# Attention with routing in front of a mixture of experts: order of VectorE's work around a tile's normalisation, and gate logits summed on GpSimd

## The chip, the cores and the metric
The kernel runs on one core of one Trainium2 chip. The metric is device time in microseconds of one execution. Before the change it was 1285.98 us, the median of three runs (1285.92 to 1286.72). Engines: TensorE (PE; PEld is its weight load), VectorE (DVE), ScalarE (ACT), GpSimd (POOL), and SyncE (SP), which issues most DMAs.

## The reference
Three stages, all in float32:

```python
k_p = k.reshape(B, H, Sp, 8, D).mean(axis=3)      # B, H, S, D = 8, 8, 576, 64
v_p = v.reshape(B, H, Sp, 8, D).mean(axis=3)      # 72 pooled keys a head
attn = softmax(q @ k_p^T / 8);  x = attn @ v_p    # -> 4608 tokens x 512
skip = x @ w_skip                                 # only tokens with skip > 0 are computed
logits = x @ w_gate                               # 8 experts, the largest one is used
x += softmax(logits)[e] * (relu(x @ w1[e]) @ w2[e])
h = x @ w_in;  out = (h * sigmoid(h)) @ w_out     # 512 -> 2048 -> 512, all tokens
```

## The kernel before
The 4608 tokens are 36 tiles of 128. Attention runs over the tiles in one software-pipelined loop (i = 0 to 35); the experts' stage then works through units of up to 384 tokens of one expert, and the feed-forward stage through blocks of 512 tokens. Each engine executes its instructions in the order in which the program writes them; nothing is reordered. So the order of the Python statements in the loop is the order of each engine's queue.

In iteration i of the loop in `attention`:

- `products(i+3)`: TensorE makes the scores of a later tile (two PSUM banks, out of a ring of four: three of the pool `hp` and one more). `ptrans(i+1)` transposes the probabilities of the next tile; ScalarE copies them to `pts`. `scores(i+3)`: VectorE takes the row maximum (`mx`, twice), ScalarE makes eight exponentials (`prb`).
- `place(1, ...)`: GpSimd issues one indirect DMA that writes 128 token numbers to their slots (`slots`). It waits for the last instruction of ScalarE, and a second one at the end of the iteration for the last one of VectorE, as a pace.
- `ready`: one entry of the list `todo`, which holds the routing in steps. An entry has a TensorE part (`count`: a few small matmuls, `rps`, that count tokens of each expert, into a bank of `hp`), a VectorE part (`step1`, 8 operations; `step2`, 9; `choose`, 6; `early`, 3), and a number (A1, A2, A3) of operations that run ahead of the tile's normalisation. The rest runs behind it.
- `pv(i)`: TensorE multiplies the probabilities with the pooled values `vex`. The result has columns for the output, for the sum of the row, and for the nine logits of each head (eight gates and the skip score), in the one PSUM buffer `pv`.
- `post(i)`: VectorE adds 1e-9 to the row sums (`sm`), inverts them, scales the logits of each head (`cc`, 8 x 9 columns) and the outputs (`x`), and sums `cc` over the heads to `lg`. When `x` is done, `pv` is free for the next tile. SP stores `x`.
- `pool_k`: VectorE sums the keys of a later batch over eight positions, in four pieces (`kp`), in the tiles that `KEYS` lists: `2: (2,3,4,4)`, `3: (6,6,7,8)`, `4: (11,12,13,13)`, `5: (15,15,16,17)`, `6: (20,20,21,22)`, `7: (24,24,25,26)`. In the tile of the last piece, `keys` has ScalarE make `kbd` of it, which the score products read.
- `self.slow`: two operations an iteration of `keep_one`, from tile 30 on, which decide on a unit that is kept.
- `pool_v`: GpSimd sums the values of a later batch over eight positions (`v`, `v`, `vp`); `router1` has TensorE transpose the sums (`vtp`); `values` has GpSimd write `vex`; `router2` has TensorE multiply with the gate weights (`cps`) and VectorE write the result to `vex`.

The tiles form groups of 9, 9, 9, 6 and 3 (`GROUP`: group, place j in it, size n). After a group's last tile the logits are stored and the group is routed (`route`), its steps spread over the next iterations. In tiles 30, 31, 32 and 35 VectorE also makes `w1l`, for the experts; after tiles 34 and 35 TensorE transposes the first unit's tokens (`xtp`) and VectorE makes `xtl`, which the first expert product `hp` reads.

In the stage `moe`, ahead of the loop over units, the first unit's tokens are copied from `xn` to `xr` by `keep()` (one of three slices on ScalarE, two on VectorE in one instruction). Behind it on VectorE stand `low2(f)`, which make `w2l`, the low halves of the second weights, for the products `yp`.

Of the kernel before, what the change touches and what calls it, by code (L numbers as in the profile page):

```python
# [5 lines left out]
F32 = mybir.dt.float32  # L6
# [7 lines left out]
ALU = mybir.AluOpType  # L14
AX = mybir.AxisListType
# [3 lines left out]
P = 128  # L19
B, H, S, D = 8, 8, 576, 64  # L20
# [3 lines left out]
E, FM = 8, 1024  # L24
# [13 lines left out]
U = 3  # L38
# [4 lines left out]
KEYS = {2: (2, 3, 4, 4), 3: (6, 6, 7, 8), 4: (11, 12, 13, 13), 5: (15, 15, 16, 17), 6: (20, 20, 21, 22),  # L43
        7: (24, 24, 25, 26)}
# [8 lines left out]
OPS = [2, 2, 2, 0, 4, 4]  # L53
ORDER = list(range(NT // 512))[::-1]
SLOW = 2
A1, A2, A3 = 8, 5, 12

C_E, C_MV, C_LID, C_WT, C_THR, C_LE, C_UN, C_PK, C_TRI = 0, 2, 13, 49, 57, 153, 217, 241, 265
C_N = C_TRI + P
# [98 lines left out]
class Kern:  # L158
# [19 lines left out]
    def attention(self, xa, rs, extra):  # L178
        nc, tc, c = self.nc, self.tc, self.c
        self.todo = todo = []  # L180
        self.slow = iter(())
        with tc.tile_pool(name="as", bufs=1) as s1, \
# [31 lines left out]
            def pool_k(b, eng, halves=(0, 2), n=2):  # L214
                k = k_t[b]
                kp = st.get((b, "k"))
                if kp is None:
                    kp = st[b, "k"] = s2.tile([P, 4, G], F32, name=f"kp_{b}", tag="kp")
                if eng is nc.vector:
                    for a in halves:  # L220
                        eng.tensor_reduce(kp[:, a:a + n], k[:, a:a + n], AX.X, ALU.add)
                else:
                    eng.tensor_tensor(k[:, :, :, 0:4], k[:, :, :, 0:4], k[:, :, :, 4:8], ALU.add)
                    eng.tensor_tensor(k[:, :, :, 0:2], k[:, :, :, 0:2], k[:, :, :, 2:4], ALU.add)
                    eng.tensor_tensor(kp, k[:, :, :, 0], k[:, :, :, 1], ALU.add)
# [98 lines left out]
            def pv(t, pt):  # L324
                ps = pp.tile([P, 1024], F32, name=f"pv_{t}", tag="pv")
                ps = ps[:, 0:H * HW].rearrange("p (h e) -> p h e", e=HW)
                for i, j, h0, n, start, stop in PVS:
                    for b, o, r, m in parts(t):
                        ve = vex[b % NB]
                        nc.tensor.matmul(ps[r:r + m, h0:h0 + n, 0:VW], pt[:CP, i, r:r + m], ve[:CP, j:j + n],  # L330
                                         start=start, stop=stop, skip_group_check=True)
                st["pv"] = ps

            def post(t):
                ps = st.pop("pv")
                xr = self.x4[:, t % 4]
                sm = s2.tile([P, H], F32, name=f"sm_{t}", tag="sm")
                cc = s2.tile([P, H, E + 1], F32, name=f"cc_{t}", tag="cc")
                nc.vector.tensor_scalar(sm, ps[:, :, D], 1e-9, None, ALU.add)
                yield  # L340
                nc.vector.reciprocal(sm, sm)
                yield
                nc.vector.tensor_tensor(cc, ps[:, :, D + 1:VW], bc(sm, 2, E + 1), ALU.mult)
                yield
                nc.vector.tensor_tensor(xr[:, 0:DM].rearrange("p (h d) -> p h d", d=D), ps[:, :, 0:D],
                                        bc(sm, 2, D), ALU.mult)
                yield
                g, j, n = GROUP[t]
                if j == 0:
                    st["lg"] = rs.tile([P, 9, E + 1], F32, name=f"lg{g}", tag="lg")  # L350
                lg = st["lg"][:, j]
                nc.vector.tensor_reduce(lg, cc.rearrange("p h e -> p e h"), AX.X, ALU.add)
                yield
                nc.sync.dma_start(xa[P * t:P * (t + 1), 0:DM], xr[:, 0:DM])
                if j == n - 1:
                    nc.sync.dma_start(xa[P * (t - j):P * (t + 1), DM:XW].rearrange("(t p) e -> p t e", p=P),
                                      st["lg"][:, 0:n, 0:E])
                    self.route(rs, g, t - j, n, st["lg"][:, 0:n])
# [30 lines left out]
            for i in range(-2, NTILE):  # L389
                if i == -2:  # L390
                    pool_v(0, ON0)
                n = 3 if i > DEEP else 2
                if i > 0 and i + n < NTILE:
                    pss = products(i + n)
                    pts[i + 1] = ptrans(i + 1, prs.pop(i + 1))
                    prs[i + n] = scores(i + n, pss)
                elif i != -1 and i <= DEEP:
                    prs[i + 2] = scores(i + 2)
                if len(self.to_place) > (3 if i < EARLY else 0) and i < NTILE - 1:
                    self.place(1, nc.scalar.last)  # L400
                extra(i, True)
                ready = todo.pop(0) if todo and i < NTILE - 1 else None
                if ready and ready[0]:
                    ready[0]()
                if i == -2:
                    values(0)
                    loadv(1)
                    loadq(1)
                if i == -1:
                    pss = products(1)  # L410
                    router1(0)
                if i == 0:
                    pv(0, pts.pop(0))
                if 0 <= i + 1 < NTILE and i + 1 not in pts:
                    pts[i + 1] = ptrans(i + 1, prs.pop(i + 1))
                if i == -1:
                    prs[1] = scores(1, pss)
                    router2(0)
                    pool_k(1, nc.vector, (0,))
                    pool_v(1, ON1)  # L420
                    values(1)
                if i > 0:
                    pv(i, pts.pop(i))
                a = ready[1]() if ready and ready[1] else iter(())
                b = post(i) if i >= 0 else iter(())
                for _ in range(ready[2] if ready else 0):
                    next(a, None)
                for _ in range(SLOW):
                    next(self.slow, None)
                for bb, tiles in KEYS.items():  # L430
                    for r, t in enumerate(tiles):
                        if i == t:
                            pool_k(bb, nc.vector, (r,), 1)
                for _ in b:
                    pass
                for _ in a:
                    pass
                for bb, tiles in KEYS.items():
                    if i == tiles[-1]:
                        keys(bb)  # L440
                if i == 0:
                    pool_k(1, nc.vector, (2,))
                    keys(1)
                for b in range(B):
                    if i + 4 == first[b] and 0 < b < B - 1:
                        loadq(b + 1)
                    if 0 <= i + 2 - first[b] < 2 and 0 < b < B - 1:
                        pool_v(b + 1, 0, ((0,), (1, 2))[i + 2 - first[b]])
                    if i + 2 == first[b]:
                        if b + 2 < B:  # L450
                            loadk(b + 2)
                            loadv(b + 2)
                    if i + 2 == first[b] + 3 + (b == 0) and b + 1 < B:
                        router1(b + 1)
                    if i + 2 == first[b] + 3 and 0 < b < B - 1:
                        values(b + 1)
                    if i + 2 == first[b] + 5 and b + 1 < B:
                        router2(b + 1)
                if i == DEEP:
                    prs[i + 3] = scores(i + 3)  # L460
                if i == EARLY + 7:
                    self.read_table(nc.sync)
                if i == 2:
                    nc.sync.dma_start(self.cb, self.con[:, P + C_TRI:])
                if i == 6:
                    self.consts()
                if i < NTILE - 1:
                    self.place(1, nc.vector.last)
                else:
                    self.place(len(self.to_place))  # L470
                extra(i)
# [373 lines left out]
    def moe(self, xa, up):  # L845
        nc, tc, c = self.nc, self.tc, self.c
        with tc.tile_pool(name="ms", bufs=1) as s1, \
             tc.tile_pool(name="mw", bufs=2) as s2, \
             tc.tile_pool(name="mp", bufs=2, space=PSUM) as pp:
            raw2, xn, xth, xtl, gi, si = self.raw2, self.xn, self.xth, self.xtl, self.gi, self.si  # L850
# [3 lines left out]
            xr = s1.tile([P, U, XW], F32, name="xr", tag="xr")  # L854
            y = self.x4[:, 0:U]

            def keep():
                nc.scalar.copy(xr[:, U - 1], xn[:, U - 1])
                nc.vector.tensor_copy(xr[:, 0:U - 1], xn[:, 0:U - 1])
# [76 lines left out]
            count, places, _ = self.todo.pop(0)  # L936
# [12 lines left out]
            def low2(f):  # L949
                nc.vector.tensor_tensor(self.w2l[:, f], raw2[:, f], self.w2h[:, f].bitcast(F32), ALU.subtract)  # L950

            keep()
            for f in range(4):
                low2(f)
            while not next(units):
# [67 lines left out]
            with tc.For_i(0, nu, 1, iteration_sync="reg_based") as u:  # L1023
                ld = lambda i, o, hi: nc.value(self.ut[0:1, i, bass.ds(u + o, 1)], hi)
                e = ld(0, 1, E - 1)
                self.load_w1(e)
                keep()
                n = ld(2, 0, U * P)
# [51 lines left out]
            for s in (2, 1):  # L1080
# [3 lines left out]
                while done:  # L1084
                    f = done.pop(0)
# [6 lines left out]
            while done:  # L1092
                f = done.pop(0)
# [560 lines left out]
```

## Time and profile before
| what | value |
|---|---|
| median of three runs | 1285.98 us (1285.92 to 1286.72) |
| the profiled execution's own time | 1285.66 us |
| its span | 1283.9 us |
| granted TensorE clock, mean | 0.997 |
| TensorE busy | 1244.5 us (97%) |
| VectorE busy | 850.9 us (66%) |
| ScalarE busy | 576.4 us (45%) |
| GpSimd busy | 354.8 us (28%) |
| attention, tiles 0 to 35 | about 19 to 151 us of the span |
| first unit of the experts' stage | about 149 to 189 us |

The profile is of one execution. Busy times are sums over instructions; an idle time carries the name of what ended it. The share over the whole span says little about attention, in which all engines are busier than on average. The chain that ended last runs through TensorE in the stages after attention.

### The profile page before, as it was taken

The numbers are of one execution on the slowest core, as the hardware profiler recorded it, in microseconds if no ns is written. First come the engines' busy times: TensorE is split into PE (matmuls) and PEld (weight loads), VectorE is DVE, ScalarE is ACT, GpSimd is POOL, SyncE is SP. The second block draws the span as 40 slices with busy tenths as digits, with TensorE's granted clock in tenths as the row PEclk, the third lists the DMA queues.
The fourth block names the chain that finished last, engine by engine and source line by source line (L and its number), as shares of the span: only waits on it lengthen the run. The fifth ranks groups of instructions, "written<-read, shape, count | busy, mean of one in ns | idle before, by whom it ended". The sixth has DMA issues, their size and how long they took to land.

```text
span 1283.9 us, 20146 instructions
## 1 busy us (share of the span) xinstructions
PE 1244.5 (97%) x6469; PEld 1058.2 (82%) x6470; DVE 850.9 (66%) x1559; ACT 576.4 (45%) x1224; POOL 354.8 (28%) x313
## 2 busy tenths in 40 slices
PE   6999899999999989999999999999999999999998
PEld 6988778998888978778888887888888888888887
DVE  5888876666776777889624245656775567846565
ACT  5877534455545554444433344433444233433321
POOL 5477432222222312223377312010201011110100
PEclk9999999999999999999999999999999999999999
DMA  9888536565765634349564225462555444462532
GB/s 372 316 299 287 194 105 236 176 202 173 241 220 187 198 113 144 140 159 305 201 246 145 85 91 174 146 213 93 178 183 186 163 141 139 148 225 94 181 118 88
DMA packets 94716, 234.45 MB, mean 183 GB/s; under 512 B 15093, under 2 KB 27509, under 8 KB 90928
## 3 DMA queue, kind: packets, MB, share of 16 engines
q1 hardware_dynamic: 87344, 216.47, 48.7%
q0 software_dynamic: 7008, 16.80, 4.0%
q8 instruction: 43, 0.70, 0.2%
q14 instruction: 33, 0.27, 0.1%
q10 hardware_dynamic: 288, 0.20, 0.0%
HBM read 183.24 MB, written 52.89 MB: 184 GB/s over the span
## 4 chain that ended last, share of the span: by engine, by line
PE 58%; DVE 2%; issue 1%; ACT 1%; POOL 0%; DMA 0%; ACTq 0%; DVEq 0%; POOLq 0%
PE yb L115 21%; PE ps L115 17%; PE fop L115 8%; PE fh L115 8%; PE hp L115 1%; PE yp L115 1%; DVE fr L115 1%; DVE ft L115 1%; PE fxp L115 1%; DVE fsg L115 0%; PE sx L115 0%; ACT fm L115 0%; DVE fgl L115 0%; ACT g L115 0%; DMA out<-fo 0%
## 5 line engine op out<-in xcount | busy, mean ns | idle before, releaser
L115 PE MATMUL yb<-wout,g 128*128 128x512 f32 x1152 | 268.5, 391 | 0.7 <-DMA wout<-wdo 0.5
L115 PEld LDWEIGHTS yb<-wout,g 128*128 128x128 f32 x1152 | 215.0, 188 | 45.6 <-DMA wout<-wdo 0.9
L115 POOL TENSOR_TENSOR tm<-tm,tm 128x512 f32<-128x512 f32 x24 | 32.2, 1340 | 411.7 <-ACT tm L115 411.7
L115 DVE TENSOR_TENSOR yacc<-yb,yacc 128x512 f32<-128x512 f32 x168 | 116.0, 691 | 38.7 <-PE yb L115 31.4
L115 ACT COPY tm<-ps 128x512 f32<-128x512 f32 x72 | 42.3, 588 | 146.4 <-PE ps L115 144.5
L115 ACT CAST g<-sg 128x512 fp32r<-128x512 f32 x96 | 59.6, 621 | 76.8 <-DVE sg L115 76.8
L115 DVE TENSOR_TENSOR fsg<-fh,fsg 128x512 f32<-128x512 f32 x48 | 33.0, 688 | 83.3 <-ACT fsg L115 80.8
L115 DVE TENSOR_TENSOR w2l<-raw,w2h 128x512 fp32r<-128x512 f32 x96 | 65.8, 690 | 29.0 <-ACT w2h L115 25.5
L115 ACT ACTIVATE hh<-hp 128x256 fp32r<-128x256 f32 (+1 forms) x96 | 39.4, 410 | 98.9 <-PE hp L115 89.2
L115 PE MATMUL fh<-w1l,fh 128*128 128x512 f32 x336 | 83.4, 390 | 0.0
L115 PE MATMUL yp<-w2h,hh 128*128 128x512 f32 x208 | 83.1, 400 | 0.0
L115 PE MATMUL yp<-w2l,hh 128*128 128x512 f32 x208 | 81.2, 391 | 1.9 <-DVE w2l L115 1.9
L115 DVE TENSOR_TENSOR tm<-ps,tm 128x512 f32<-128x512 f32 x24 | 16.6, 691 | 98.1 <-PE ps L115 98.1
L115 PE MATMUL yp<-w2h,hl 128*128 128x512 f32 x208 | 81.3, 391 | 0.0
L115 PE MATMUL hp<-xth,w1h 128*128 128x256 f32 (+2 forms) x384 | 72.5, 311 | 6.6 <-PEq L1650 3.3
L115 PE MATMUL hp<-xtl,w1h 128*128 128x256 f32 (+2 forms) x384 | 72.0, 308 | 3.1 <-DVE xtl L115 1.9
L115 PEld LDWEIGHTS fh<-w1l,fh 128*128 128x128 f32 x336 | 62.8, 188 | 12.9
L115 PE MATMUL hp<-xth,w1l 128*128 128x256 f32 (+2 forms) x384 | 71.2, 308 | 0.0
L115 ACT ACTIVATE prb<-s,mx 128x72 f32<-128x72 f32 x288 | 65.3, 355 | 11.0 <-DVE mx L115 11.0
L115 DVE TENSOR_TENSOR g<-sg,g 128x512 fp32r<-128x512 f32 x96 | 65.8, 686 | 5.1 <-ACT g L115 4.8
L115 PEld LDWEIGHTS hp<-xth,w1h 128*128 128x128 f32 x384 | 60.4, 192 | 9.4 <-issue 7.6
L115 PE MATMUL fop<-fh,fgh 128*128 128x512 f32 x168 | 66.4, 395 | 1.2 <-ACT fgh L115 1.2
(240 smaller groups left out, 2723.1 us busy)
## 6 DMA issues: line engine op xcount, KB each, us to landing
raw<-w SPq DMA_DIRECT2D x88, 512.0 KB, 4.4
wout<-wdo SPq DMA_DIRECT2D x48, 512.0 KB
win<-wdi SPq DMA_DIRECT2D x36, 512.0 KB
w1l<-wdi SPq DMA_DIRECT2D x36, 512.0 KB
xa<-x SPq DMA_DIRECT2D x36, 256.0 KB
fx<-xa SPq DMA_DIRECT2D x9, 1024.0 KB
v<-vR SPq DMA_DIRECT2D x7, 1280.0 KB
fr<-w_in SPq DMA_DIRECT2D x16, 512.0 KB
```

What stands on the lines that cost most here:

```text
L115: ins = f(*a, **k)
```

## The change
Six things change: the numbers of routing operations ahead of a normalisation (A1 from 8 to 5, A2 from 5 to 0, A3 from 12 to 5; a number above the step's length means all of it); the sum of the logits over the heads, which in the tiles j < n - 2 of the groups of 9 and 6 is made by three additions on GpSimd, in place, with four `cc` buffers for two; the place of `count`, behind `pv(i)` instead of ahead of it; the place of a tile's second key reduction, behind the normalisation; the place of the slow operations, behind the rest of the routing step; and the copy ahead of the first unit, all three slices on ScalarE (the later calls of `keep` stay).

```diff
-A1, A2, A3 = 8, 5, 12
+A1, A2, A3 = 5, 0, 5
@@ post(t)
-                cc = s2.tile([P, H, E + 1], F32, name=f"cc_{t}", tag="cc")
+                cc = s2.tile([P, H, E + 1], F32, name=f"cc_{t}", tag="cc", bufs=4)
@@
-                nc.vector.tensor_reduce(lg, cc.rearrange("p h e -> p e h"), AX.X, ALU.add)
+                if j < n - 2 and n > 3:
+                    g2 = nc.gpsimd
+                    g2.tensor_tensor(cc[:, 0:4], cc[:, 0:4], cc[:, 4:8], ALU.add)
+                    g2.tensor_tensor(cc[:, 0:2], cc[:, 0:2], cc[:, 2:4], ALU.add)
+                    g2.tensor_tensor(lg, cc[:, 0], cc[:, 1], ALU.add)
+                else:
+                    nc.vector.tensor_reduce(lg, cc.rearrange("p h e -> p e h"), AX.X, ALU.add)
@@ the loop over tiles
                 ready = todo.pop(0) if todo and i < NTILE - 1 else None
-                if ready and ready[0]:
-                    ready[0]()
@@
                 if i > 0:
                     pv(i, pts.pop(i))
+                if ready and ready[0]:
+                    ready[0]()
                 a = ready[1]() if ready and ready[1] else iter(())
                 b = post(i) if i >= 0 else iter(())
                 for _ in range(ready[2] if ready else 0):
                     next(a, None)
+                todays = [(bb, r) for bb, tiles in KEYS.items() for r, t in enumerate(tiles) if i == t]
+                for bb, r in todays[:1]:
+                    pool_k(bb, nc.vector, (r,), 1)
+                for _ in b:
+                    pass
+                for bb, r in todays[1:]:
+                    pool_k(bb, nc.vector, (r,), 1)
+                for _ in a:
+                    pass
                 for _ in range(SLOW):
                     next(self.slow, None)
-                for bb, tiles in KEYS.items():
-                    for r, t in enumerate(tiles):
-                        if i == t:
-                            pool_k(bb, nc.vector, (r,), 1)
-                for _ in b:
-                    pass
-                for _ in a:
-                    pass
@@ moe, ahead of the first unit
-            keep()
+            for j in range(U):
+                nc.scalar.copy(xr[:, j], xn[:, j])
```

## Rows read from the trace of the kernel before

**Rows 1.** Busy time by stretch (us, PE, PEld, DVE, ACT, POOL; clock; DMA)
```profile
35.00:71.00 36.00, 35.66 (x299) 33.39 (x296) 31.50 (x108) 29.99 (x122) 18.16 (x19) 1.00 0.89 312
```

**Rows 2.** TensorE's waits, 17 to 162 us (total, times, longest)
```profile
PE pv L115 <- DVE x L115: 7.0, 8, 1.8
```

**Rows 3.** Timeline of TensorE (start, us, what, idle before)
```profile
55.29 0.38 PE L115 MATMUL rps<-rohb,onesb 128*128 128x72 bf16 x9
55.92 1.63 PE L115 MATMUL pv<-vex,pts 120*128 120x148 f32 x10 [0.24 <-DVE x L115]
...
76.94 1.63 PE L115 MATMUL pv<-vex,pts 120*128 120x148 f32 x10 [0.93 <-DVE x L115]
...
88.38 1.63 PE L115 MATMUL pv<-vex,pts 120*128 120x148 f32 x10 [0.73 <-DVE x L115]
...
95.43 1.63 PE L115 MATMUL pv<-vex,pts 120*128 120x148 f32 x10 [0.67 <-DVE x L115]
```

**Rows 4.** Timeline of VectorE, tiles 18 and 20
```profile
86.45 0.25 DVE L115 TENSOR_TENSOR roh<-req,rm 128x72 f32<-128x72 f32 x1
...
86.97 0.16 DVE L115 TENSOR_SCALAR sm<-pv 128x8 f32<-128x8 f32 x1
...
92.71 1.40 DVE L115 TENSOR_REDUCE kp<-k 128x72 f32<-128x576 f32 x2
```

**Rows 5.** Timeline, tile 4: ScalarE, VectorE
```profile
38.02 1.09 ACT L115 ACTIVATE kbd<-kp,consts 128x288 f32<-128x288 f32 x2
...
38.06 0.28 DVE L115 TENSOR_REDUCE lg<-cc 128x9 f32<-128x72 f32 x1
```

**Rows 6.** Timeline of VectorE, tile 10
```profile
56.60 0.15 DVE L115 TENSOR_TENSOR tot<-tot,rps 128x8 f32<-128x8 f32 x1
...
57.58 0.17 DVE L115 TENSOR_SCALAR sm<-pv 128x8 f32<-128x8 f32 x1
...
58.17 0.68 DVE L115 TENSOR_TENSOR x<-pv,sm 128x512 f32<-128x512 f32 x1
...
59.52 0.82 DVE L115 TENSOR_REDUCE mx<-s 128x4 f32<-128x288 f32 x2
```

**Rows 7.** Timeline of GpSimd and TensorE, value sums of batches 4 and 6
```profile
62.09 0.99 POOL L115 DMA_INDIRECT slots<-consts,ix  x1 [1.12 <-ACT prb L115]
...
70.11 0.86 POOL L115 TENSOR_TENSOR vp<-v 120x320 f32<-120x320 f32 x1
...
71.09 0.47 PE L115 MATMUL vtp<-ident,vp 120*128 120x120 f32 x3
...
94.53 0.97 POOL L115 DMA_INDIRECT slots<-consts,ix  x1 [1.19 <-ACT prb L115]
...
102.53 0.87 POOL L115 TENSOR_TENSOR vp<-v 120x320 f32<-120x320 f32 x1
...
104.20 0.47 PE L115 MATMUL vtp<-ident,vp 120*128 120x120 f32 x3
```

**Rows 8.** Groups of GpSimd instructions up to 165 us (busy, mean ns)
```profile
L115 POOL TENSOR_TENSOR vex<-vp,consts 120x128 f32<-120x128 f32 x32 | 12.2, 402 | 3.9 <-PE pv L115 3.7
...
L115 POOL TENSOR_SCALAR vex<-consts 128x11 f32<-128x11 f32 x3 | 0.8, 264 | 6.9 <-DMA consts<-con 6.8
...
L115 POOL MEMSET tot<- 128x8 f32 x1 | 0.1, 104 | 0.0
```

**Rows 9.** Timeline of VectorE, tiles 15 and 24
```profile
75.52 0.17 DVE L115 TENSOR_SCALAR sm<-pv 128x8 f32<-128x8 f32 x1 [0.73 <-PE s L115]
...
107.88 0.46 DVE L115 TENSOR_REDUCE mx<-s 128x4 f32<-128x288 f32 x1 [1.67 <-PE pv L115]
```

**Rows 10.** Timeline after tile 34: VectorE, TensorE
```profile
147.83 1.02 DVE L115 TENSOR_TENSOR xtl<-xtp,xth 128x384 fp32r<-128x384 f32 x2
...
152.12 0.91 PE L115 MATMUL hp<-xtl,w1h 128*128 128x384 f32 x2 [1.10 <-DVE lg L115]
```

**Rows 11.** Timeline of the first unit: VectorE, TensorE
```profile
168.07 0.68 DVE L115 COPY xr<-xn 128x1040 f32<-128x1040 f32 x1
...
173.66 0.50 PE L115 MATMUL yp<-w2l,hh 128*128 128x512 f32 x1 [1.22 <-DVE w2l L115]
```

## The prediction
> **What bounds the kernel now.** I read the chain of waits first: it ends in 58% TensorE, all of it after 470 us, where the feed-forward stages run TensorE back to back. Nothing of the change stands there, so it can only move the whole rest to the left or right. The busy times by stretch show where: between 35 and 71 us, the middle of attention, TensorE is busy 35.66 of 36 us, VectorE 31.50, ScalarE 29.99 and GpSimd 18.16 [rows 1]. TensorE's own waits come next: only one group counts, eight times the `pv` products waited for `x`, the normalised tile, 7.0 us in all [rows 2]. `pv` has one PSUM buffer, so the products of tile i+1 wait until VectorE has run `sm`, reciprocal, `cc`, `x` of tile i (1.27 us in a row, 57.58 to 58.85 in [rows 6]). Where something stands ahead of those four on VectorE, TensorE pays. Four of the eight are in [rows 3]; others are in tile 24 and in the last three tiles, where no score products are left to fill the time. That is all that the reordering can win in the middle of attention: about 3.3 us. For what it can lose I looked at ScalarE, GpSimd and the TensorE rows that follow a GpSimd result [rows 5, 7].
>
> **The change part by part.** I follow the lag of TensorE against before, in us, tile by tile (plus is late). The sum goes against the profiled execution, 1285.66 us (span 1283.9 and 1.76 around it); the median of the runs shown lies 0.32 higher.
>
> *Second key reduction behind the normalisation.* In tile 4 both of batch 2's last reductions stand before the normalisation and fill VectorE's wait for `pv`; ScalarE makes `kbd` from them at 38.02 [rows 5]. After, the second (half of a 1.40 us pair, as in [rows 4]) starts where `lg` stood, at 38.06, and ends at 38.8. `kbd` is 0.8 late, and the exponentials queued behind it, whose banks the next score products need. Between 0 and 0.8; I take the middle. Lag 0.45. Tile 13 has the same order; what it costs there is covered by the stall below.
>
> *Routing, group 0.* Eight operations of the first routing step stand before tile 9's normalisation, now five; the counting matmuls go behind `pv`. So `pv` of tile 10 no longer waits 0.24 [rows 3] and no longer has the 0.4 us of counting matmuls [rows 3] ahead: lag 0.45 - 0.65 = -0.2. But step 2 of the routing had five operations in the shadow of `pv` (56.60 to 57.58, [rows 6]; `sm` then started when `pv` was done, so they cost nothing). Now all nine follow the normalisation: the score maximum at 59.52 comes 0.98 later, less 0.19 for the `lg` that is gone. And the counts' PSUM bank, out of the ring that the score products use, stays taken until the second operation of step 2 has read it, now behind the normalisation: I work out 0.6 us of wait for the next score products, with 0.4 for the counting matmuls moved behind. Lag 0.8 at tile 11.
>
> *Logit sums on GpSimd.* The condition takes 25 tiles (7, 7, 7 and 4 of the groups), with three additions each of 36, 18 and 9 elements a partition. VectorE loses 0.19 us of its queue per tile. No such addition is in the trace. From below: a memset of 8 elements, 104 ns, so 0.31 for three. From above: the 128-element product, 402 ns, so 1.21. I take the operation on 11 elements, 264 ns, as nearest in size: 0.8 a tile [rows 8]. GpSimd has idle time over the stage, but not where it counts. Batch 4's value sums are queued behind slot writes in one unbroken run from 62.09 to 70.97, and TensorE's transposes of that result start at 71.09, directly behind `pv`: 0.12 us of slack [rows 7]. The additions of tiles 11 and 12 come into that run: 1.6 us. Its start is the slot write that waits for tile 14's exponentials, 0.5 later through the late score maximum. So the sums end at 73.07 and TensorE, due at 71.9 with its lag, waits 1.2. Lag 2.0. Queued behind the transposes are score products, hence everything of tile 15.
>
> The Trainium skill, GPSIMD Engine Reference, section 3.1 Elementwise, speaks against the move: an addition of two tensors costs about 2.6 cycles an element there and about twice VectorE's time in all, so elementwise work belongs on VectorE. This case's rows have 402 ns for 128 elements and 264 ns for 11, so here most is a fixed price for each instruction, which is paid three times. By a plain factor of two on the 0.27 us `lg`, a tile would cost 0.54 as an estimate, and the sum would end near 1286.4.
>
> *Tile 15.* `pv` waited 0.93 for `x` [rows 3], because `sm` started 0.73 us after the reductions, on a late signal of TensorE [rows 9]. No moved operation stands in that gap; with TensorE itself late, the wait may be absorbed or repeat. I count half: lag 1.5.
>
> *Group 1.* Three of eight operations fewer before tile 18's normalisation: `sm` moves from 86.97 to 86.45 [rows 4], 0.5 of the 0.73 wait. The counting matmuls, which stood in that wait, now cost 0.3. In tile 20 one of two reductions goes behind: 0.66 of the 0.67 wait, but step 2 has put five operations (0.98, less 0.19) ahead of it; the rest of that wait goes as TensorE is late anyway: -0.3. Lag 1.0 at tile 21.
>
> *Batch 6's value sums.* The same run again: slot write at 94.53, sums done at 103.40, transposes at 104.20, 0.8 of slack [rows 7]. The start is 1.3 later (lag and step 2), two tiles' additions are 1.6: 106.3 against TensorE's 105.2. Wait 1.1, lag 2.1.
>
> *Tile 24 to the end of attention.* Before, VectorE got its score maximum 1.67 late [rows 9], then did two reductions, and TensorE waited. One reduction goes behind (0.66), and TensorE's own lateness may swallow the rest, up to 2.0. I take 1.3: lag 0.8. Tile 28 gains 0.45 as tile 18 did; in tiles 30 and 31 the two slow operations now stand ahead of `vex`, for which `pv` waits: 0.35 lost. Lag 0.7. In the tail VectorE is busy from tile 34's normalisation to the `xtl` that TensorE's first expert product waits for (1.10 us) [rows 10]. Five operations of step 2 (0.9) and two slow ones (0.35), all once in the wait for `pv`, join that stretch; about 0.35 comes back earlier, where the slow pair and three routing operations no longer stand before tiles 32 and 33. Lag 1.6.
>
> *Copy in the first unit.* The VectorE copy at 168.07 holds its queue 0.61 us; right behind it stand the `w2l` halves, for which TensorE waits up to 1.22 [rows 11]. VectorE is what limits there, so 0.61 comes off. ScalarE gets two copies more (0.6 each); what it does next, `hh` of the last slice, is read by VectorE 4 us later: nothing. With that cover gone it would cost at most 0.6.
>
> Four `cc` buffers are just enough that VectorE never waits for the sums: at most some 5 us of GpSimd work stands ahead of one, against three tiles' time of about 10. The logits' DMA on SP's queue follows a group's last tile, whose sum stays on VectorE.
>
> Sum: 1285.66 + 0.45 - 0.65 + 1.0 + 1.2 - 0.5 - 0.5 + 1.1 - 1.3 - 0.1 + 0.9 - 0.61, about 1286.66; against the median 1287.0. (From 1.5 to 1.0 at group 1 is -0.5 + 0.3 - 0.3.)
>
> **The rivals.** *The reordering wins and GpSimd keeps up* (faster). If an addition costs near 0.1 us, the two runs of [rows 7] end only 0.6 later each, and TensorE's waits on them are small; the gains of [rows 3] stay: 0.65 + 0.5 + 0.66 + 0.66 + 0.45, and 0.61 in the first unit, less 0.9 in the tail: -2.7, so about 1283.3. For it: 7.0 us of waits on `x` [rows 2]. Against: the smallest arithmetic on GpSimd takes 264 ns.
>
> *GpSimd's queue sets the pace* (slower). The place is the transposes of batches 4 and 6. At the upper price, 1.21 and some 0.08 between dependent additions, a tile costs 1.4; the two runs then end 1.2 later again each than I take, and the late signals of [rows 9] come back instead of being absorbed (0.5 and 0.7 lost of what I counted). 1287.0 + 1.2 + 1.2, up to 1290. It decides from about 1.1 us a tile. For it: 0.12 us of slack; against: 0.8 at the second run.
>
> *A wash by another way*: the late signals move with the instruction order, and tile 4's and the bank's price are half of mine: 1286.0 to 1286.4; within the forecast's range.
>
> **How the numbers follow.** About 0.2% (2.6 us) is what a measurement of this kernel can tell from no change. Forecast, own range 1285.2 to 1288.8: 0.46. Faster rival 0.25, slower rival 0.29. Faster by over 0.2% (under 1283.4): most of its rival, 0.24. Slower by over 0.2% (above 1288.5): most of its rival and the upper edge of the forecast, 0.30. Within: 0.46. The range reaches from the faster rival's time to the slower one's: 1283.3 to 1290.2.
>
> **What would show it.** GpSimd rows of `lg` near 0.25 us each and TensorE waiting on `vp` before the transposes near 72 and 105 us; no waits of `pv` for `x` in tiles 10, 19 and 21 over 0.3; a score product waiting on the counts' bank near 58; `w2l` 0.6 earlier against the last `hp`. No wait on `vp` at all would make the forecast wrong on the fast side; waits over 2 us there, or VectorE waiting in `cc`, on the slow side.

## The result, and the profile after

The changed kernel takes 1296.19 us (median of four runs, 1294.35 to 1296.92) against 1285.95 (four runs, 1283.8 to 1286.72): ratio 1.0078, 95% interval [1.0063, 1.0092]. A second comparison, that of e5 below, gave 1.0065 [1.0043, 1.0087], with 1294.63 against 1288.46 us. So it is slower, by 6 to 10 us as the medians differ; 1287.0 was forecast, with 1290.2 as the upper end. A ratio and the quotient of the two medians differ by up to 0.002 here, and the interval covers both. One run of the kernel before, of 2533 us, is left out of the ratios of e1 to e4.

TensorE's waits in the kernel after, 17 to 165 us (total, times, longest), which answer to [rows 2]; the last two lines are of the kernel before, over the same stretch:

```profile
PE vtp L115 <- POOL vp L115: 3.9, 2, 2.4
PE pv L115 <- DVE x L115: 2.5, 3, 1.2
PE pv L115 <- DVE roh L115: 1.9, 1, 1.9
PE hp L115 <- DVE pick L115: 1.8, 1, 1.8
PE pv L115 <- issue: 1.2, 1, 1.2
PE pv L115 <- DVE vex L115: 1.2, 1, 1.2
...
PE pv L115 <- PE pt L115: 0.9, 1, 0.9
...
PE pv L115 <- DVE vex L115: 0.5, 1, 0.5
PE pv L115 <- issue: 0.3, 1, 0.3
```

By name the wait for `x` fell from 7.0 to 2.5 us, as the reordering meant it to. But a wait is named after what ended last: `pv` of tile 19 needs `x` as before and now waits 1.85 us under the name of `roh`, and in the last tiles the names changed too. All waits of `pv` together are 7.8 us before and 7.7 after (8.5 in the second profile of the changed kernel, e5). So the reordering took nothing off them in sum, and the 3.9 us on the value sums are new. In the timeline of TensorE after (start, us, what, idle before), against [rows 3, 7, 10]:

```profile
76.40 0.53 PE L115 MATMUL vtp<-ident,vp 120*128 120x120 f32 x3 [1.51 <-POOL vp L115]
93.75 2.52 PE L115 MATMUL pv<-vex,pts 120*128 120x148 f32 x10 [1.85 <-DVE roh L115]
113.96 0.53 PE L115 MATMUL vtp<-ident,vp 120*128 120x120 f32 x3 [2.42 <-POOL vp L115]
163.32 0.91 PE L115 MATMUL hp<-xtl,w1h 128*128 128x384 f32 x2 [1.78 <-DVE pick L115]
```

The additions themselves cost what was taken for them: GpSimd's groups, 0 to 165 us (count | busy, mean ns), the three that are new beside [rows 8]:

```profile
L115 POOL TENSOR_TENSOR cc<-cc 128x36 f32<-128x36 f32 x25 | 6.7, 270 | 18.5 <-DVE cc L115 18.2
L115 POOL TENSOR_TENSOR cc<-cc 128x18 f32<-128x18 f32 x25 | 6.5, 261 | 2.0
L115 POOL TENSOR_TENSOR lg<-cc 128x9 f32<-128x9 f32 x25 | 5.0, 201 | 1.9
```

That is 0.73 us a tile. What they set off was not foreseen. In tile 18 the first routing step runs on VectorE. Two of its operations on 72 elements, 0.45 and 0.32 us before, are now long; GpSimd's value sum, which the logit sums have pushed to this place, runs beside them (VectorE before, VectorE after, GpSimd after):

```profile
85.18 0.45 DVE L115 TENSOR_TENSOR req<-lg,rmx 128x72 f32<-128x72 f32 x1
85.66 0.32 DVE L115 TENSOR_TENSOR req<-req,consts 128x72 f32<-128x72 f32 x1
...
89.69 0.87 DVE L115 TENSOR_TENSOR req<-lg,rmx 128x72 f32<-128x72 f32 x1
90.60 1.57 DVE L115 TENSOR_TENSOR req<-req,consts 128x72 f32<-128x72 f32 x1
...
87.56 2.91 POOL L115 TENSOR_TENSOR v<-v 120x1280 f32<-120x1280 f32 x1
90.54 1.54 POOL L115 TENSOR_TENSOR v<-v 120x640 f32<-120x640 f32 x1
```

The first ends at 90.56 and the addition beside it at 90.47; the second ends at 92.17, its addition at 92.08. Then `pv` of tile 19 waits its 1.85 us. In tile 23 the same happens to the choice, on 8 elements (VectorE before, VectorE after, GpSimd after):

```profile
103.42 0.17 DVE L115 TENSOR_TENSOR sc<-tot,sc 128x8 f32<-128x8 f32 x1
...
104.03 0.17 DVE L115 TENSOR_TENSOR m<-sc 128x8 f32<-128x8 f32 x1
...
110.62 1.27 DVE L115 TENSOR_TENSOR sc<-tot,sc 128x8 f32<-128x8 f32 x1
112.33 1.61 DVE L115 TENSOR_TENSOR m<-sc 128x8 f32<-128x8 f32 x1
...
110.33 1.54 POOL L115 TENSOR_TENSOR v<-v 120x640 f32<-120x640 f32 x1
112.02 0.99 POOL L115 DMA_INDIRECT slots<-consts,ix  x1 [0.15 <-DVE sc L115]
113.03 0.87 POOL L115 TENSOR_TENSOR vp<-v 120x320 f32<-120x320 f32 x1
```

`sc` ends at 111.89 with the addition (111.87). `m` starts beside the slot write and ends at 113.94 with the addition that follows it (113.90). The slot write itself waited for VectorE's `sc`, and behind it stands `vp`, for which the transposes wait 2.42 us. The two engines hold each other up.

The granted clock differs as well. These windows (us, busy times of PE, PEld, DVE, ACT, POOL, clock, DMA) are of the kernel after; in that of before the first has clock 1.00, and no stretch between 10 and 355 us is below full speed:

```profile
15.00:23.00 8.00, 7.91 (x32) 6.78 (x31) 2.72 (x9) 4.96 (x23) 4.23 (x5) 0.57 1.01 425
94.00:98.00 4.00, 4.00 (x28) 3.85 (x28) 2.41 (x11) 2.31 (x10) 0.79 (x4) 0.57 1.08 321
```

TensorE runs there mostly at 1.2 instead of 2.4 GHz: at the start, which the change does not touch, and behind the waits of 1.85 and 2.42 us (near 94 and 115 us). The experiments had to say which of these belong to the change.

### The profile page after: what moved, and what is told of

Its sections match the earlier page's. It is cut to its first block, busy times and chain, and to the rows that moved or that the text cites. A ratio compares the mean times of both kernels' runs of the same rounds, so it can differ in the third digit from the quotient of the medians.

```text
span 1294.9 us, 20220 instructions
## 1 busy us (share of the span) xinstructions
PE 1250.9 (97%) x6469; PEld 1063.7 (82%) x6470; DVE 849.5 (66%) x1533; ACT 578.0 (45%) x1226; POOL 375.5 (29%) x388
## 4 chain that ended last, share of the span: by engine, by line
PE 59%; DVE 2%; ACT 1%; issue 1%; POOL 0%; DMA 0%; ACTq 0%; POOLq 0%; DVEq 0%
PE yb L115 21%; PE ps L115 17%; PE fh L115 9%; PE fop L115 9%; PE hp L115 1%; PE yp L115 1%; DVE ft L115 1%; PE fxp L115 1%; DVE fr L115 0%; PE sx L115 0%; DVE fsg L115 0%; DVE fgl L115 0%; ACT g L115 0%; ACT fm L115 0%; DMA out<-fo 0%
## 5 line engine op out<-in xcount | busy, mean ns | idle before, releaser
L115 ACT ACTIVATE fsg<-fh 128x512 f32<-128x512 f32 x48 | 28.7, 597 | 89.7 <-PE fh L115 86.3
```

What stands on the lines that cost most here:

```text
L115: ins = f(*a, **k)
```

## The experiments

The expectations name three theories. Q: the logit sums make GpSimd's queue late, and TensorE waits for its results. O: the moved operations themselves cost the time. C, from e5 on: value sums pushed late by Q run beside VectorE's operations and hold them (a collision). The experiments ran on four chips, and each ratio is against the kernel before on the same one: its median was 1289.1 us for e1 to e4 (30 runs), 1288.5 for e5 to e8 (12), 1285.3 for e9 to e12 (17) and 1285.6 for e13 (one run).

In the table, "lag" is the start of `pv` of a tile less its start in the profile of before, less the lag at tile 2 (given as "start"), because the start varies from one execution to the next, by -1.13 to 2.01 us, also for one program. "First unit" is the same for the `yp` product at 173.66 of [rows 11]. A star: a stretch at 1.2 GHz lies between the start and this point, and part of the lag is its.

| profile | start | 6 | 11 | 15 | 16 | 19 | 24 | 25 | 35 | first unit |
|---|---|---|---|---|---|---|---|---|---|---|
| after | 1.94 | 0.74 | 0.93 | 3.43 | 2.50 | 3.44 | 8.89* | 7.68* | 7.47* | 8.29* |
| after again (e5) | -0.43 | 0.74 | 0.94 | 3.44 | 2.51 | 3.44 | 7.00 | 5.14 | 5.33 | 6.04 |
| before again (e6) | 1.83 | 0.02 | 0.00 | 0.01 | 0.01 | 0.01 | 0.02 | 0.03 | 0.06 | 1.27* |
| all sums on VectorE (e1) | 1.92 | 0.87 | 1.13 | 2.12 | 1.24 | 0.60 | 1.03 | 1.55 | 1.88 | 3.77* |
| before + sums (e2) | -0.11 | -0.03 | 0.01 | 2.27 | 1.34 | 3.28 | 4.67 | 2.80 | 4.63 | 5.02* |
| sums in 13 tiles (e3) | -0.23 | 0.75 | 1.17 | 2.22 | 1.28 | 0.22 | 0.66 | 1.14 | 0.97 | 3.19* |
| before + fills (e4) | 2.01 | 0.03 | -0.01 | 4.04* | 3.65* | 3.69* | 5.94* | 4.00* | 5.86* | 5.88* |
| value sums early (e7) | -0.10 | 0.74 | 0.94 | 2.48 | 1.55 | 2.99 | 3.89 | 2.30 | 3.93 | 6.33* |
| e7, routing later (e13) | -1.12 | 0.74 | 0.96 | 2.50 | 1.57 | 0.65 | 6.19* | 4.33* | 7.24* | 9.50* |
| first sum early (e9) | -0.25 | 0.74 | 0.95 | 2.59 | 1.66 | 2.99 | 7.08* | 5.73* | 4.87* | 6.86* |
| step 2 ahead (e8) | -1.13 | 0.86 | 1.09 | 2.29 | 1.40 | 0.77 | 1.32 | 1.86 | 7.29* | 6.67* |
| keys alone (e11) | -0.66 | 0.86 | 0.70 | 1.60 | 0.60 | 0.74 | 0.11 | -1.76 | -2.32 | -2.64 |
| routing alone (e12) | 0.10 | 0.02 | 0.41 | 0.51 | -0.32 | -0.83 | 0.26 | -1.46 | -1.65 | -1.03 |
| 13 tiles, before's order (e10) | 0.48 | -0.03 | 0.02 | 0.03 | -0.80 | -1.15 | -1.14 | -2.90 | -4.52 | -5.45 |

Two profiles of one program agree to 0.06 us from tile 6 on wherever the clock is full (the kernel before to tile 35, the changed kernel to tile 19). So a lag in this table is read to a tenth of a us, while run times spread by 11 us.

**The order or the sums (e1, e2).** First the changed kernel with every sum on VectorE:

```diff
-                if j < n - 2 and n > 3:
+                if False:
```

> The changed kernel with every logit sum back on VectorE; all reorderings and the ScalarE copies stay. Theory Q (GpSimd's queue): the sums make the value sums of batches 4 and 6 late (TensorE waited 1.5 and 2.4 us for vp), move them beside routing operations of VectorE that then take 0.9 to 1.6 us in place of 0.2, and TensorE's clock falls to half for 3.4 us behind two of these stalls; so without the sums most of the 10 us goes: 1286 to 1288, no wait on vp, no VectorE operation of the routing over 0.5 us. Rival O (order): the moved operations themselves cost it (late kbd in tile 4, nine operations behind the normalisation, tail); then it stays at 1292 or more.

1293.17 us, ratio 1.0033 [1.0014, 1.0052]: about 4 us over the 1289.1 of this chip. Q expected next to nothing, O the whole loss (its 1292 was set against 1286); it is neither. No wait on the value sums is left, and tile 35 lags 1.88 us. The value sum of tile 18 now runs from 82.29 to 86.82, and the two operations behind it, at 88.34 and 88.83, take 0.45 and 0.33 us.

Then the kernel before with the sums alone (the `if` of the change and the four buffers):

> The kernel before with the 25 sums on GpSimd and four cc buffers, nothing else. Q: most of the loss is here, 1292 to 1296, with TensorE waiting on vp near 72 and 105 us. O: under 1289, since the order is the old one.

1293.48 us, ratio 1.0030 [1.0009, 1.0051]. The transposes wait again, and so does VectorE, in an order that is otherwise that of before:

```profile
PE vtp L115 <- POOL vp L115: 3.3, 2, 2.1
...
87.37 1.57 DVE L115 TENSOR_TENSOR req<-req,consts 128x72 f32<-128x72 f32 x1
```

Neither half alone is the change. By the lags the sums weigh more (4.6 against 1.9 us at tile 35); the run times, 1.0030 and 1.0033, don't tell the halves apart.

**Where the sums are, and what they are (e3, e4).** The changed kernel with GpSimd's sums only in tiles 0 to 6, 9, 18 and 27 to 30, where no value sum stands close behind:

```diff
-                if j < n - 2 and n > 3:
+                if j < n - 2 and n > 3 and (t < 10 or t == 18 or t > 26):
```

> The changed kernel with GpSimd's sums only in tiles 0 to 9, 18 and 27 to 30 (13 of 25), where no slot writes are queued ahead of value sums. Q: what counts is the place in the queue, so nearly all of the gain of the run without any sums comes: within 1.5 us of it. If the sums cost by their number (GpSimd's load, the wait for cc), about half of the gain: 1290 to 1291. O: no gain.

1292.64 us, ratio 1.0024 [1.0007, 1.0042]. Tile 35 lags 0.97, less than the 1.88 with all sums on VectorE: by this pair of profiles a sum on GpSimd costs nothing where nobody waits for GpSimd. The run times are too close to say so. And the kernel before with three fills in place of three sums (the sums stay on VectorE as well):

```diff
+                if j < n - 2 and n > 3:
+                    for _ in range(3):
+                        nc.gpsimd.memset(self.fill, 0.0)
```

> The kernel before, sums on VectorE as they were, and in the same 25 tiles three fills of 208 elements on GpSimd (about 0.27 us each), which read nothing and wait for nothing of VectorE. Q (time in the queue alone): slower by 4 to 9 us, vp late near 72 and 105 us. If the loss comes from GpSimd waiting for cc, or from its reads: within 1.5 us of before.

1294.85 us, ratio 1.0046 [1.0027, 1.0064]. A fill took 277 ns, and the transposes wait in the same two places:

```profile
PE vtp L115 <- POOL vp L115: 4.8, 2, 2.8
```

So it is the time in GpSimd's queue, not the addition, that makes the value sums late. The value sums hold VectorE here too: `req` of tile 18 takes 0.76 us.

**Both kernels once more (e5, e6).**

> The changed kernel itself once more, on the chip of the runs beside it, for a second profile. Theory Q (GpSimd's queue) and theory C (the value sums, pushed late, hold VectorE's operations with two inputs in SBUF, and the granted clock falls behind TensorE's waits) both expect the two waits of the transposes on the value sums again, 1.5 and 2.4 us in the first profile, and the long operations of the routing in tile 18 (0.87 and 1.57 us) and of the choice in tile 23 (1.27 and 1.61 us). If these are chance, they are not there a second time. The start (TensorE at 1.2 GHz from 15.7 to 22.5 us, 1.9 us lost) is taken for chance: it may come or not. Time 1.006 to 1.009 of the kernel before.

1294.63 us, ratio 1.0065 [1.0043, 1.0087]. The waits of 1.51, 1.85 and 2.43 us are all there; no stretch at 1.2 GHz follows them. So these waits and the long operations belong to the program; the clock behind them does not always fall.

> The kernel before once more, for a second profile of it. What both profiles of it show belongs to the kernel, what only one shows is chance. Expected: no wait of TensorE on the value sums, VectorE's routing operations in tile 18 at 0.45 us at most; the stretches at 1.2 GHz near 359 and 472 us of the span again, and possibly others (near the start, near 150 and 223 us), which the first profile did not have.

1293.51 us for the same program that took 1285.66 (12 other runs of it on this chip took 1283.32 to 1294.29). Every lag from tile 6 to 35 is within 0.06 us, but it has two slow stretches that the first profile has not (windows as above):

```profile
155.00:158.40 3.40, 3.40 (x12) 3.40 (x11) 1.57 (x8) 1.00 (x2) 2.37 (x4) 0.50 0.87 237
223.00:227.00 4.00, 4.00 (x16) 3.93 (x15) 1.81 (x3) 1.00 (x2) 1.05 (x1) 0.57 0.00 0
```

They and the start make 6.2 of its 7.8 us, by 234 us of the span; where the other 1.6 arise stays open. At the start (1.83 us) TensorE's rows are long, 2.29 us for score products that took 1.25 and 2.42 for a `pv` that took 1.55, but the granted clock on record is 1.00 there. The profile on which the prediction rests has neither of these.

**Against the late value sums (e7, e9).** The changed kernel with the value sums one tile earlier:

```diff
-                    if 0 <= i + 2 - first[b] < 2 and 0 < b < B - 1:
-                        pool_v(b + 1, 0, ((0,), (1, 2))[i + 2 - first[b]])
+                    if 0 <= i + 3 - first[b] < 2 and 0 < b < B - 1:
+                        pool_v(b + 1, 0, ((0,), (1, 2))[i + 3 - first[b]])
```

> The changed kernel, its value sums on GpSimd issued one tile earlier. Theory Q: the two waits of the transposes on the value sums (1.5 and 2.4 us) go, and with them nearly all that the logit sums cost: tile 35 lags 3 to 4 us less than in the changed kernel, the time comes to 1.003 to 1.004 of the kernel before, as with all sums on VectorE. Theory C: the same waits go, and the routing operations of tile 18 and the choice in tile 23 are back at 0.2 to 0.45 us only if the sums no longer run beside them; where they do, VectorE still takes 0.8 to 1.6 us for one of them and pv behind it waits over 1 us. A rival: the earlier sums wait for the values' transfer, and nothing is gained.

1294.15 us, ratio 1.0035 [1.0006, 1.0063], which is the time that Q expected. Both waits on the value sums are gone, and the choice's operations take 0.17 us each, with no addition beside them. But tile 18's routing now meets two of the sums (VectorE, GpSimd, TensorE's wait):

```profile
86.70 2.04 DVE L115 TENSOR_TENSOR req<-lg,rmx 128x72 f32<-128x72 f32 x1
88.78 0.90 DVE L115 TENSOR_TENSOR req<-req,consts 128x72 f32<-128x72 f32 x1
...
86.09 0.99 POOL L115 DMA_INDIRECT slots<-consts,ix  x1
87.11 1.54 POOL L115 TENSOR_TENSOR v<-v 120x640 f32<-120x640 f32 x1
88.72 0.86 POOL L115 TENSOR_TENSOR vp<-v 120x320 f32<-120x320 f32 x1
...
PE pv L115 <- DVE roh L115: 2.4, 1, 2.4
```

But only 1.4 of 5.3 us came back at tile 35, where Q expected 3 to 4. With only the first step early:

> The changed kernel, only the first step of each value sum (the 2.9 us addition) one tile earlier on GpSimd; the other two steps stay where they are. Lags are against the profile of the kernel before, less the lag at tile 2. Theory Q: both waits of the transposes on the value sums go; nothing else moves; tile 35 at 5.3 - 1.5 - 2.4 + up to 1, so 1.4 to 2.4. Theory C: in tile 18 no value sum runs beside the routing any more, so its operations take 0.45 us or less, pv behind it waits under 0.7 instead of 1.85 us and tile 19 lags 1.0 to 1.6 (3.44 in the changed kernel, 2.99 with all three steps early); in tile 23 the later steps still run beside the choice, so one of its operations takes 0.5 to 1.6 us, where with all three steps early each took 0.17.

1294.75 us (two runs), ratio 1.0073 [1.0044, 1.0102]. Theory Q missed: waits of 0.65 and 1.81 us on the value sums stayed. Theory C missed too in tile 18: the later steps moved up with the first, met the routing, and `req` took 1.95 us. In tile 23 it held: `m` took 1.60 us again. The test did not separate the theories, so a last one moved the routing instead of the sums.

**The routing one tile later (e13).** The kernel of e7, with:

```diff
+        if g == 1:
+            todo.append((None, None, 0))
         todo.append((None, step1, A1))
@@
-            todo += [(None, None, 0)] * 3 + [(None, lambda: self.choose(new), A3)]
+            todo += [(None, None, 0)] * 2 + [(None, lambda: self.choose(new), A3)]
```

> The kernel with all value sums one tile early, and the two routing steps of the second group one tile later (tiles 19 and 20); the choice and all that follows stay in their tiles. So the value sums of batch 5 (83.0 to 89.6 us of the span in that kernel) end about where the first routing step now begins. Theory C (VectorE's operation is held until GpSimd's addition beside it has ended): the two operations that took 2.04 and 0.90 us take 0.25 to 0.45 us, pv of tile 19 does not wait for them, and tile 19 lags 0.6 to 1.2 us, where it was 2.99; the price may come back one tile later, where the second step meets the products for vex. Rival: the sums cost at tile 19 because TensorE or VectorE has one more late result there, whatever runs beside it; then tile 19 lags 2.5 us or more.

1296.91 us, one run. Tile 19 lags 0.65 instead of 2.99 us. The first step's operations are short; in tile 20 the second step meets batch 6's sums, and its operations on 9 elements are long (the first line is of the kernel before):

```profile
91.61 0.17 DVE L115 SCALAR_TENSOR_TENSOR pf<-sb,pf 128x9 f32<-128x9 f32 x1
...
88.66 0.27 DVE L115 TENSOR_TENSOR req<-lg,rmx 128x72 f32<-128x72 f32 x1
...
96.71 1.53 POOL L115 TENSOR_TENSOR v<-v 120x640 f32<-120x640 f32 x1
96.73 1.54 DVE L115 SCALAR_TENSOR_TENSOR pf<-sb,pf 128x9 f32<-128x9 f32 x1
98.32 0.86 POOL L115 TENSOR_TENSOR vp<-v 120x320 f32<-120x320 f32 x1
98.38 0.82 DVE L115 SCALAR_TENSOR_TENSOR ix<-sl,pf 128x9 int32<-128x9 f32 x1
```

A score product then waits 2.51 us. The price went where the collision went: theory C is shown for tile 19. In the rows shown, each held operation starts while GpSimd is at work and ends within 0.1 us of the end of one of its tensor operations. Two of them, `m` of 1.61 us and `req` of 2.04 us in e7, start beside a slot write and end with the addition that follows it, so a held operation can also lose more than one GpSimd instruction. The Trainium skill, SBUF — State Buffer, section Who interferes with whom, states the rule: a VectorE instruction with two inputs in SBUF contends with a GpSimd instruction that reads SBUF, and the one that issues first holds the other for its whole length. The trace agrees, with 1.54 us for an operation that else takes 0.17.

**Parts of the order (e8, e11, e12).** The kernel of e1 with five operations of step 2 and the slow pair ahead:

> The changed kernel with all logit sums on VectorE, five operations of the second routing step ahead of the normalisation as in the kernel before, and the two slow operations ahead too. What stays of the change: five instead of eight operations of the first step ahead, the counting matmuls behind pv, the second key reduction behind, the copies on ScalarE. Theory O (the order costs by what it adds behind the last normalisations): TensorE's wait at the first expert product falls from 1.8 to about 1.1 us as before, tile 35 lags 1 us less than with all sums on VectorE (3.8, of which 1.9 at the start is chance), and the time is 0.999 to 1.001 of the kernel before. Rival: the order loses by the late key reduction in tile 4 and the counts; then tile 35 still lags over 1.5 us net of the start.

1293.29 us, ratio 1.0055 [1.0033, 1.0077]. The first expert product no longer waits, but theory O missed in the sum: with `count` behind `pv`, step 2 ahead makes the normalisation wait for the counts (2.37 us at tile 34), and `pv` of tile 35 waits 2.94 us for `x`. A slow stretch at 112.7 us adds to its time. Next, the kernel before with the second key reduction behind:

> The kernel before with the second key reduction of a tile behind the normalisation, nothing else. As the late keys of tile 4 are the only part that acts before tile 9, the lag at tile 6 should be 0.74 as in the changed kernel (I had predicted 0.45); after that, gains of up to 0.66 at tiles 21 and 25, none at tile 35: 0 to 0.7 late there. Rival: the lag at tile 6 comes from the order of the score products, and this kernel shows none.

1283.85 us, one run. Tile 6 lags 0.86 and tile 15 another 0.89, where tile 13 has the same order. The end at -2.32 was not expected (0 to 0.7 was). Two late signals of the kernel before, described below, are gone here: the lag falls by 1.00 at tile 16 and by 1.87 at tile 25, more than the whole of it. And with the routing alone:

> The kernel before with the routing alone as in the changed kernel (five, none and five operations ahead of the normalisation, the counting matmuls behind pv); sums, keys, slow operations and copies as before. Theory O: no lag at tile 6, -0.6 at tile 10 and 0.2 to 0.4 at tile 11 (the counts' bank and the score maximum come late), -0.5 at tile 19; in the tail the first expert product waits 1.5 to 1.8 us instead of 1.1. If the lags at tiles 11 and 12 of the changed kernel are GpSimd's, they are not here.

1289.38 us, one run. Tile 10 at -0.57, tile 11 at 0.41, tile 19 at -0.83 and a first expert product that waits 1.8 us, about as expected; tile 12 lags hardly more than tile 11 (0.50), so the 0.77 that the changed kernel loses there is GpSimd's.

**A better version (e10).** The kernel before with the sums on GpSimd in the 13 tiles of e3 and the copies on ScalarE:

> The kernel before, in its own order, with the logit sums on GpSimd in 13 tiles only (0 to 6, 9, 18, 27 to 30), where no value sum stands close behind them, and with the three copies ahead of the first unit on ScalarE. From the pair of runs with all sums on VectorE and with these 13 on GpSimd, tile 35 should come 0.9 us earlier, and the copies gave 0.97 us in the profile of the changed kernel: the first w2l product comes 1.9 us earlier than before, net of the start. As a time that is 0.998 to 1.000; the difference may be too small for the runs. Theory Q and theory C agree on it; if GpSimd's additions cost something wherever they are, tile 35 comes later than before.

1283.06 us (12 runs), ratio 0.9985 [0.9972, 0.9999]: about 2 us faster than the kernel before, with an interval that all but reaches 1, and clearly faster than the changed kernel. Its trace is 5.45 us ahead in the first unit, not 1.9. Of the surplus, 0.83 and 1.76 us come at tiles 16 and 25, where this kernel no longer has the late signals of [rows 9]; e11 and e12, without the sums, gain there too, so that part is not the sums'. How much of the 2 us is the sums' is not shown: e11, which has none, was at -2.64 in the first unit. The wait for `x` is 4.0 us here, against [rows 2].

## Why the prediction was wrong

By the profile without slow stretches in attention (e5), the program lost 6.04 us up to the first unit, where I had summed to 1.0. Step by step, forecast and measured (us):

| step | forecast | measured |
|---|---|---|
| late keys, to tile 6 | +0.45 | +0.74 |
| tile 10 | -0.65 | -0.58 |
| tile 11 | +1.0 | +0.78 |
| tile 12 | 0 | +0.77 |
| value sums of batch 4, to tile 15 | +1.2 | +1.73 |
| tile 15's late signal | -0.5 | -0.93 |
| tiles 17 to 21 | -0.5 | +1.85 |
| value sums of batch 6, to tile 24 | +1.1 | +2.64 |
| tile 24's late signal | -1.3 | -1.86 |
| to tile 31 | -0.1 | +1.40 |
| tail to the first `hp` wait | +0.9 | +0.47 |
| copies | -0.61 | -0.97 |

The failed step is *Logit sums on GpSimd*. Its price was right (0.73 us and gaps against 0.8), its two places were right (waits of 1.51 and 2.42 us on `vp` where 1.2 and 1.1 were forecast). It counted GpSimd's time against GpSimd's queue only, and put at nothing that later value sums run beside other work of VectorE. That gave tile 19 (about 1.6 us more than with the sums on VectorE, shown by e13), most probably tile 12 (`pi`, `pf`, `ix` of step 2 at 0.45, 0.33, 0.32 and 0.26 instead of 0.17 us beside a 2.01 us run of `vex`), and part of the second `vp` wait, to which the held `sc` added through the slot write. It was to be seen beforehand: the routing operations at 0.45 and 0.32 us beside 0.22 to 0.25 of their neighbours, in the very trace that I read.

Most of the step from tile 25 to 31 is the same collision, by rows of e5: 1.12 us come at tile 28, behind two operations that took 0.18 and 0.17 us before (VectorE, then GpSimd):

```profile
124.19 0.68 DVE L115 TENSOR_TENSOR sc<-table,m 128x24 f32<-128x24 f32 x1 [0.36 <-DMA table<-slots]
...
125.12 0.67 DVE L115 TENSOR_SCALAR g<-table 128x3 int32<-128x3 f32 x1
...
120.29 4.54 POOL L115 TENSOR_TENSOR v<-v 120x1280 f32<-120x1280 f32 x2
124.91 0.86 POOL L115 TENSOR_TENSOR vp<-v 120x320 f32<-120x320 f32 x1
```

In e2, e4 and e7, where both are long too, tile 28 loses 1.4 to 2.0 us against tile 25; in e1, e3, e10, e11 and e12, where both are short, 0.23 at most. No run moved this collision by itself.

"Group 1" was right as an order: without the sums on GpSimd (e1), tile 19 gains 0.64 us. "Tile 13 ... is covered by the stall below" held only because the `vp` wait covers the same time: without that wait it costs 0.89 us (e11) and 0.90 (e1). Of the gains of [rows 3], that of tile 10 came, and that of `pv` at 76.94 too, as the late signal of tile 15 is gone. In tile 19 the wait grew to 1.85 us, and in tile 21 it is 0.56, or 1.15 in e5, where 0.67 was to go. The first expert product's longer wait came (1.10 to 1.78 us), and so did the copies' gain: a `w2l` wait of 0.69 us at 169.41 in the kernel before is gone, though the 1.22 us one of [rows 11] stayed at 1.21.

The order was mispriced too. The forecast without its two waits on value sums stands at -1.6 us at tile 31, where e1 lags 2.68. Of the difference of 4.3, 1.8 are tile 24's late signal, which e1 keeps; 0.9 come at tile 15, as in e11, where the prediction counted on the stall; and 1.2 lie between tiles 25 and 31, where e1 and e12 lose 1.1, with a longer wait for `vex` (1.19 and 1.18 us, 0.53 before). One sum in the prediction is off by itself: with 0.54 instead of 0.8 us a tile, its two waits are about 0.5 us shorter each, which gives about 1286.0 and not 1286.4.

The slower rival had the right place, its price was too low, and it rested on a dearer addition, which was not the reason. What goes beyond these 6 us I can't give to the change: between the first two profiles lie 11.0 us, of which 6.0 are the program's, 1.9 the start, 2.3 two slow stretches in attention, 0.8 later. Whether the longer waits bring slow stretches more often stays open: the second profile of the changed kernel has one at 222.7 us, the second of the kernel before has four and the start.

## What to carry to other kernels

Before work moves to GpSimd, list which VectorE operations on SBUF operands will run beside it and beside everything that it pushes back; a held operation costs at least the rest of GpSimd's instruction, however small it is itself. Move only where no result of GpSimd is awaited soon: with 13 well-placed sums tile 35 came 0.9 us earlier than with none (e3, e1), with all 25 it came over 3 us later (e5, e1). A wait has the name of what ended last, so compare the waits of a product in sum. And profile a program twice before a sum in tenths of a us is made against one execution's time.

## What the runs showed of the hardware

An operation of VectorE on 9 elements took 1.54 us beside a GpSimd addition (e13), and 0.17 in the kernel before; in the other direction two GpSimd additions `cc`, 0.56 us elsewhere, took 1.59 us beside VectorE's `w1l` on 1024 elements (at 143.39 us of the kernel after).

The same program, profiled twice, differed by 7.8 us with the same waits in attention: 4.3 us lie in two stretches where the granted clock fell to 1.2 GHz, 1.8 at the start, where it was 1.00 on record. And one wait of 1.85 us was followed by 1.2 GHz in one execution and not in another.

The late signals of [rows 9], where VectorE stands idle 0.73 and 1.67 us although the product that it waits for has ended by the profile, came back to 0.01 us in the second profile of the kernel before, and went, or were covered, in most kernels whose order differs anywhere (-0.8 to -1.0 at tile 16, -1.4 to -1.9 at tile 25; e1, e3 and e8 keep the second). By the two profiles of the kernel before they belong to a build, not to chance; their cause was not tried.
